# A new order table and named rooms for two kinds of turning tiles in an attention and gated feed-forward kernel

## The chip, the cores and the metric

The kernel runs on one core of a Trainium2 chip. The metric is the device time of one launch in microseconds, as the median of several executions. In the rows, PE is the matrix engine, PEld its weight loads, DVE the vector engine, ACT the scalar engine, POOL the GpSimd engine, and SP the engine that only issues transfers here (its transfers stand as SPq).

## The reference

Attention over keys and values that are averaged in groups of eight, and then a gated feed-forward layer on its output:

```
k_p = k.reshape(B, H, Sp, 8, D).mean(axis=3)      # B = H = 8, S = 576, D = 64, Sp = 72
v_p = v.reshape(B, H, Sp, 8, D).mean(axis=3)
attn = softmax(q @ k_p^T / sqrt(D))
x = (attn @ v_p) as 4608 tokens x 512
out = (sigmoid(x @ w_gate) * (x @ w_val)) @ w_out  # 512 x 1536, 512 x 1536, 1536 x 512, all float32
```

## The kernel before

The 4608 tokens are nine blocks of 512. Every float32 product is made of three products of a high and a low half (fp32r), so each operand is split: ACT copies the high half, DVE subtracts it from the original for the low one. The weights come from memory as 64-bit numbers, 1 MB for each of twelve pieces, and are converted on the chip by ACT and DVE (`to_f32`: two ACT steps w<-raw and raw<-raw, then DVE steps on w, then the split into `parts`).

The first pass (block 0's whole path, and the attention of blocks 1 and 2) is written out by hand in the string `ORDER`; it fills the first 140 us or so and converts all the weights on the way. After it come four rounds of two blocks each. A round makes gate and value products by a scheme of seven block products instead of eight (`hidden`, tiles `chain`), multiplies them into `h`, and makes the output products in the same way (`second_sums`, tiles `acc`). The attention of later blocks (`attention`: scores `sc`, exponentials `e`, transposes `tp`, products with the values `av`) is slipped in between, as tasks.

What is written is not issued at once: a `Book` records each instruction, or each group that must stay together, as one of 3800 numbered units. At the end the loop over the string `LATER` issues the units in the order of the numbers in it, and each engine gets its own share of them in that order. An engine works through its share strictly in turn, so a unit that has to wait holds up all that stand behind it on that engine. Tiles carry the dependencies: an instruction waits for what it reads, and the first write to a room waits for the last reader of what was there.

Two kinds of tiles turn in rings. `raw` tiles (128 x 576 float32, the landing place of keys, queries and values) come from the pool `rawp` with three rooms, in `load` (L593) and at the start of `first_pass`. `y` tiles (128 x 512 float32; gates of the first blocks in `gate` and `gated`, sums in `product`, outputs `o` in `result`) come from `two`, with two rooms for the tag `y`. A ring hands its rooms out in rotation, in the order in which the tiles are recorded. All recorded instructions carry the line of the recording helper, L317 (L320 after the change), so the rows are told apart by their tiles.

Of the kernel before, what the change touches and what calls it, by code (L numbers as in the profile page):

```python
# [11 lines left out]
F32 = mybir.dt.float32  # L12
# [7 lines left out]
P = 128  # L20
# [90 lines left out]

LATER = """
# [217 lines left out]
def attention_then_ffn(ctx: ExitStack, tc: tile.TileContext, qT, kT, vm, vr, vn, sums8, wgv, wo, const, out, outT):  # L330
# [34 lines left out]
    def split(h, l, x):  # L365

        nc.scalar.copy(h, x)
        nc.vector.tensor_tensor(out=l, in0=x, in1=h.bitcast(F32), op=ALU.subtract)

    kept = {
        (kind, p, g): dram.tile([P, 2, 2 * HALF], F32R, name=f"kept{kind}{p}{g}")
# [1204 lines left out]
```

## Time and profile before

| what | before |
| --- | --- |
| median of three runs | 906.28 us (904.79 to 907.96) |
| profiled execution, its own time | 906.25 us |
| its span, first to last instruction | 904.5 us |
| PE busy | 893.6 us (99%), 4162 matmuls |
| PEld, DVE, ACT, POOL busy | 81%, 73%, 55%, 22% |
| granted clock of PE | 1.000 in all slices |
| bytes moved | 237.56 MB, 263 GB/s over the span |

The time of the run is 1.75 us more than the span: this lies ahead of the first instruction and behind the last. A row of the profile gives the start, the length, the engine, the tile written and the tiles read, and in brackets the idle time of that engine just before it and what ended it. The ends of matmuls are modelled, and matmuls overlap, so a short stall of PE shows less idle time than it costs; the distance between the starts of two rows shows all of it.

### The profile page before, as it was taken

The numbers are of one execution on the slowest core, as the hardware profiler recorded it, in microseconds if no ns is written. First come the engines' busy times: TensorE is split into PE (matmuls) and PEld (weight loads), VectorE is DVE, ScalarE is ACT, GpSimd is POOL, SyncE is SP. The second block draws the span as 40 slices with busy tenths as digits, with TensorE's granted clock in tenths as the row PEclk, the third lists the DMA queues.
The fourth block names the chain that finished last, engine by engine and source line by source line (L and its number), as shares of the span: only waits on it lengthen the run. The fifth ranks groups of instructions, "written<-read, shape, count | busy, mean of one in ns | idle before, by whom it ended". The sixth has DMA issues, their size and how long they took to land.

```text
span 904.5 us, 12612 instructions
## 1 busy us (share of the span) xinstructions
PE 893.6 (99%) x4162; PEld 735.1 (81%) x4162; DVE 657.4 (73%) x1039; ACT 497.1 (55%) x1071; POOL 199.4 (22%) x369
## 2 busy tenths in 40 slices
PE   7999999999999999999999999999999999999998
PEld 6788778888888888888888888888888888888886
DVE  7989788889899998757678796356589552224863
ACT  5888887587856475445365554334355542224352
POOL 2412101011164235443343104132213000000000
PEclk9999999999999999999999999999999999999999
DMA  9899888889999888787987787686747775746644
GB/s 342 302 332 349 289 331 303 299 280 330 329 328 313 278 288 287 234 304 260 302 273 245 243 279 260 225 269 198 256 127 249 247 251 201 227 169 205 195 167 141
DMA packets 100289, 237.56 MB, mean 263 GB/s; under 512 B 13856, under 2 KB 34720, under 8 KB 98688
## 3 DMA queue, kind: packets, MB, share of 16 engines
q1 hardware_dynamic: 85040, 203.84, 66.7%
q0 software_dynamic: 15040, 32.79, 10.6%
q8 instruction: 33, 0.54, 0.2%
q14 instruction: 32, 0.26, 0.1%
q10 hardware_dynamic: 144, 0.13, 0.0%
HBM read 176.02 MB, written 60.69 MB: 262 GB/s over the span
## 4 chain that ended last, share of the span: by engine, by line
PE 90%; DVE 4%; DMA 3%; ACT 2%; issue 1%; SPq 0%; DVEq 0%; ACTq 0%
PE chain L317 55%; PE acc L317 27%; PE av L317 4%; PE sc L317 3%; DVE early L317 1%; DMA raw<-in_wgv 1%; DMA raw_o<-in_wo 1%; PE tp L317 1%; DMA raw<-in_vr 1%; DMA h<-in_kT 0%; ACT e L317 0%; DVE s L317 0%; DVE hs L317 0%; DVE h L317 0%; ACT hs L317 0%
## 5 line engine op out<-in xcount | busy, mean ns | idle before, releaser
L317 PE MATMUL chain<-xo,parts 128*128 128x512 f32 x2316 | 543.7, 392 | 0.0
L317 PEld LDWEIGHTS chain<-xo,parts 128*128 128x128 f32 x2316 | 430.7, 188 | 92.5 <-issue 1.0
L317 PE MATMUL acc<-hs,oparts 128*128 128x512 f32 x1008 | 237.3, 391 | 0.3 <-issue 0.2
L317 PEld LDWEIGHTS acc<-hs,oparts 128*128 128x128 f32 x1008 | 188.0, 188 | 40.9 <-issue 1.2
L317 POOL DMA_DIRECT2D turned<-turn x240 | 131.7, 551 | 214.8 <-DVE turn L317 185.2
L317 DVE TENSOR_TENSOR y<-chain,sV 128x512 f32<-128x512 f32 x46 | 31.1, 686 | 69.3 <-PE chain L317 59.0
L317 DVE TENSOR_TENSOR hs<-h,hs 128x1024 fp32r<-128x1024 f32 x52 | 63.0, 1217 | 11.6 <-ACT hs L317 11.4
L317 ACT CAST hs<-h 128x1024 fp32r<-128x1024 f32 x52 | 54.4, 1050 | 30.0 <-PE acc L317 23.1
L317 ACT COPY chain<-chain 128x512 f32<-128x512 f32 x46 | 26.4, 576 | 57.0 <-PE chain L317 47.3
L317 DVE TENSOR_TENSOR y<-chain,sG 128x512 f32<-128x512 f32 x46 | 31.2, 682 | 34.0 <-PE chain L317 23.4
L317 ACT CAST hs<-s 128x1024 fp32r<-128x1024 f32 x36 | 37.5, 1051 | 28.4 <-PE acc L317 13.0
L317 ACT COPY sG<-chain 128x512 f32<-128x512 f32 x46 | 26.7, 586 | 46.5 <-PE chain L317 44.8
L317 DVE TENSOR_TENSOR hs<-s,hs 128x1024 fp32r<-128x1024 f32 x36 | 43.8, 1219 | 11.2 <-ACT hs L317 10.9
L317 ACT COPY sV<-chain 128x512 f32<-128x512 f32 x46 | 26.7, 585 | 38.8 <-PE chain L317 36.1
L317 DVE SCALAR_TENSOR_TENSOR h<-gate,chain 128x512 f32<-128x512 f32 x46 | 30.6, 677 | 21.8 <-PE chain L317 21.7
L317 ACT ACTIVATE gate<-chain 128x512 f32<-128x512 f32 x46 | 26.9, 594 | 34.2 <-PE chain L317 31.7
L317 PE MATMUL sc<-kbd,raw 128*128 128x144 f32 (+1 forms) x262 | 41.2, 296 | 0.1
L317 PEld LDWEIGHTS sc<-kbd,raw 128*128 128x128 f32 (+1 forms) x262 | 33.6, 176 | 7.9 <-issue 2.8
L317 ACT ACTIVATE gate<-y 128x512 f32<-128x512 f32 x46 | 28.9, 633 | 19.1 <-DVE y L317 19.0
L317 PE MATMUL acc<-oparts,hs 128*128 128x512 f32 x144 | 38.7, 402 | 0.2 <-ACT oparts L317 0.2
L317 DVE TENSOR_REDUCE m<-sc 128x4 f32<-128x288 f32 x48 | 21.7, 452 | 18.2 <-PE sc L317 17.7
L317 DVE SCALAR_TENSOR_TENSOR h<-gate,y 128x512 f32<-128x512 f32 x46 | 31.0, 683 | 0.3
(211 smaller groups left out, 1073.8 us busy)
## 6 DMA issues: line engine op xcount, KB each, us to landing
oparts<-keptS SPq DMA_DIRECT2D x48, 512.0 KB, 4.4
oparts<-keptO SPq DMA_DIRECT2D x72, 256.0 KB, 4.2
raw<-in_wgv SPq DMA_DIRECT2D x12, 1024.0 KB, 8.5
out<-o SPq DMA_DIRECT2D x35, 256.0 KB, 3.6
raw<-in_kT SPq DMA_DIRECT2D x28, 288.0 KB, 5.0
raw<-in_qT SPq DMA_DIRECT2D x29, 256.0 KB, 4.7
raw<-in_vm SPq DMA_DIRECT2D x24, 256.0 KB, 5.6
raw_o<-in_wo SPq DMA_DIRECT2D x12, 512.0 KB, 8.1
```

Source lines behind the costliest of these rows:

```text
L317: return self._book.take(lambda: f(*args, **named))
```

## The change

The table `LATER` is replaced by another order of the same 3800 units. 707 of PE's 916 units stand at another place of PE's sequence, 922 of 1039 on DVE, 828 of 942 on ACT, 300 of 348 on POOL and 483 of 555 on SP; the mean move is 2.7, 4.7, 4.3, 2.7 and 3.6 places, the largest 43. No instruction is added, removed or resized.

Two strings now say which room a turning tile gets. `RAWS` has 77 digits for three rooms, and names the same room twice in a row 24 times; `YS` has 132 digits for two rooms, and does so 46 times. The rooms are as many and as large as before.

```
+RAWS = (
+    "12001221110021020122201202110021110020221001211220110020012211020100211102"
+)
+YS = (
+    "0101011001011001010101011100011000101010101000100110101110100111010110101100011110111010011001011011"
+    "10110010000110101001101001011101"
+)
 LATER = """
-6 5 4 7 0 11 3 2 21 8 25 27 19 28 14 18 23 31 22 20 9 26 13 35 17 36 33 1 10 40 45 76 39 37 12 48 47 52 16 55 32 66 38
...
+6 2 21 27 4 28 35 5 19 7 26 11 0 3 18 8 9 13 14 31 39 25 20 23 17 22 36 66 10 40 45 52 1 33 32 67 48 53 12 62 58 76 38
...
-    cpool, work, two = sb("cpool"), sb("work"), sb("two", 2)
-    rawp, wpool, opool = sb("rawp", 3), sb("wpool"), sb("opool")
+    cpool, work, two, ypool = sb("cpool"), sb("work"), sb("two", 2), sb("ypool")
+    rawp, wpool, opool = sb("rawp"), sb("wpool"), sb("opool")
...
+    raws, ys = iter(RAWS), iter(YS)
+
+    def raw_tile():
+        return rawp.tile([P, S], F32, name="raw", tag=f"raw{next(raws)}")
+
+    def y_tile(name):
+        return ypool.tile([P, BT], F32, name=name, tag=f"y{next(ys)}")
...
-        return fill(rawp.tile([P, S], F32, name="raw"), *what)
+        return fill(raw_tile(), *what)
...
-            y = two.tile([P, BT], F32, name="y", tag="y")
+            y = y_tile("y")
...
-        gate = two.tile([P, BT], F32, name="y", tag="y")
+        gate = y_tile("y")
...
-                t = two.tile([P, BT], F32, name="o", tag="y")
+                t = y_tile("o")
...
-        rooms += [rawp.tile([P, S], F32, name="raw") for _ in range(3)]
+        rooms += [raw_tile() for _ in range(3)]
...
-            ygate[f] = two.tile([P, BT], F32, name="y", tag="y")
+            ygate[f] = y_tile("y")
```

Three places of the new order matter below. The numbers behind tile names count buffers and are higher by three after the change.

The first is ACT's sequence in the first pass, around the conversion of an output weight (w_o and raw_o, then its high half oparts). The rows `e` are the exponentials of block 2, `hs` is the high half of block 0's h. Before:

```order
L317 ACTIVATE y<-chain 128x512
L317 ACTIVATE e,early<-sc,early 128x72
L317 ACTIVATE w_o<-raw_o 128x1024
L317 ACTIVATE e,early<-sc,early 128x72
L317 ACTIVATE raw_o<-raw_o,cst 128x1024
L317 ACTIVATE e,early<-sc,early 128x72 x5
L317 CAST hs<-h 128x1024
L317 ACTIVATE e,early<-sc,early 128x72 x4
L317 CAST oparts<-w_o 128x2x512
```

After:

```order
L320 ACTIVATE e,early<-sc,early 128x72 x4
L320 ACTIVATE y<-chain 128x512
L320 CAST vh_100<-early 64x64
L320 ACTIVATE w_o<-raw_o 128x1024
L320 ACTIVATE e,early<-sc,early 128x72 x2
L320 ACTIVATE raw_o<-raw_o,cst 128x1024
L320 CAST hs<-h 128x1024
L320 ACTIVATE e,early<-sc,early 128x72 x2
L320 CAST oparts<-w_o 128x2x512
```

The tanh of a gate (y<-chain), one copy of values (vh) and four exponentials now stand ahead of the conversion's first step, and between hs and oparts two exponentials are left of four.

The second is ACT's sequence some 40 rows later, where the last gate and value weights are converted (w_394 and raw_382 before are w_397 and raw_385 after; w_396 and raw_384 are the value weight's). Before:

```order
L317 CAST parts<-w_379 128x2x256
L317 ACTIVATE w_394<-raw_382 128x1024
L317 ACTIVATE raw_382<-raw_382,cst 128x1024
L317 ACTIVATE y<-chain 128x512
L317 CAST parts<-w_394 128x2x256 x2
L317 ACTIVATE y<-chain 128x512
L317 ACTIVATE kbd_91<-ks 64x72
L317 ACTIVATE w_396<-raw_384 128x1024
```

After:

```order
L320 ACTIVATE y<-chain 128x512 x2
L320 ACTIVATE w_397<-raw_385 128x1024
L320 ACTIVATE raw_385<-raw_385,cst 128x1024
L320 ACTIVATE kbd_94<-ks 64x72
L320 ACTIVATE w_399<-raw_387 128x1024
L320 CAST parts<-w_397 128x2x256
L320 ACTIVATE raw_387<-raw_387,cst 128x1024
L320 CAST other<-early 96x64
```

Both gates now stand ahead of the conversion of the gate weight, and the second step of its split (parts<-w_397) is moved behind the first two steps of the value weight and more.

The third is PE's sequence in the first round, where the products av of block 3's second pair follow the transposes tp of their probabilities pm. Before:

```order
L317 MATMUL tp<-cst,pm 128x128 x4
L317 MATMUL chain<-xo_459,parts 128x512 x6
L317 MATMUL chain<-xo_453,parts 128x512 x6
L317 MATMUL chain<-xo_467,parts 128x512 x6
L317 MATMUL chain<-xo_424,parts 128x512 x6
L317 MATMUL chain<-xo_416,parts 128x512 x6
L317 MATMUL av<-ph,vh_98 128x192
L317 MATMUL av<-pl,vh_98 128x192
L317 MATMUL av<-ph,vl_103 128x192
L317 MATMUL av<-pr,vres_108 128x192
L317 MATMUL av<-ph,vh_97 128x320
```

After:

```order
L320 MATMUL tp<-cst,pm 128x128 x4
L320 MATMUL chain<-xo_419,parts 128x512 x6
L320 MATMUL chain<-xo_420,parts 128x512 x6
L320 MATMUL chain<-xo_427,parts 128x512 x6
L320 MATMUL sc<-kbd_94,raw 128x144 x2
L320 MATMUL av<-ph,vh_101 128x192
L320 MATMUL av<-pl,vh_101 128x192
L320 MATMUL av<-ph,vl_106 128x192
L320 MATMUL av<-pr,vres_111 128x192
L320 MATMUL chain<-xo_419,parts 128x512 x6
L320 MATMUL av<-ph,vh_100 128x320
```

One more group of six chain matmuls and two score groups stand ahead of the first of the av rows, fewer of the others between the transposes and it.

## Rows read from the trace of the kernel before

**Rows 1.** The page, busy time, share of the span and count of each engine

```profile
PE 893.6 (99%) x4162; PEld 735.1 (81%) x4162; DVE 657.4 (73%) x1039; ACT 497.1 (55%) x1071; POOL 199.4 (22%) x369
```

**Rows 2.** Busy time by stretches: stretch, its length, each engine, clock, DMA share, GB/s

```profile
0.00:20.00 20.00, 15.75 (x82) 13.39 (x82) 14.93 (x37) 10.77 (x25) 3.67 (x22) 1.00 0.94 332
20.00:100.00 80.00, 79.40 (x390) 64.17 (x390) 72.01 (x121) 67.47 (x174) 21.08 (x29) 1.00 0.91 323
...
320.00:880.00 560.00, 559.98 (x2552) 462.38 (x2552) 364.37 (x522) 254.16 (x442) 123.45 (x225) 1.00 0.72 238
```

**Rows 3.** PE's timeline, the start-up

```profile
9.74 1.25 PE L317 MATMUL sc<-kbd,h 128*128 128x144 f32 x8 [1.16 <-ACT kbd L317]
...
14.72 0.55 PE L317 MATMUL tp<-cst,early 128*128 128x128 f32 x3 [0.92 <-DVE early L317]
...
20.42 0.63 PE L317 MATMUL tp<-cst,early 128*128 128x128 f32 x4 [0.57 <-DVE r L317]
```

**Rows 4.** PE's timeline, 98 to 101 us

```profile
98.44 0.65 PE L317 MATMUL sc<-kbd,raw 128*128 128x144 f32 x4
99.03 0.76 PE L317 MATMUL sc<-kbd,raws 128*128 128x144 f32 x4
99.97 1.19 PE L317 MATMUL acc<-oparts,hs 128*128 128x512 f32 x4 [0.18 <-ACT oparts L317]
```

**Rows 5.** ACT's timeline, 92 to 96 us

```profile
92.78 1.13 ACT L317 ACTIVATE w_o<-raw_o 128x1024 f32<-128x1024 f32 x1 [1.94 <-DMA raw_o<-in_wo]
...
95.24 0.30 ACT L317 ACTIVATE e<-sc,early 128x72 f32<-128x72 f32 x1
```

**Rows 6.** Timelines of PE and ACT, 105 to 110 us

```profile
105.50 0.59 ACT L317 COPY xs<-av 128x512 f32<-128x512 f32 x1
...
105.62 0.26 PE L317 MATMUL tr<-identr,r 128*96 128x128 f32 x1 [0.16 <-ACT early L317]
...
109.08 0.69 PE L317 MATMUL acc<-oparts,hs 128*128 128x512 f32 x2
109.91 0.76 PE L317 MATMUL sc<-kbd,raw 128*128 128x144 f32 x4
```

**Rows 7.** PE's timeline, 110 to 124 us

```profile
110.85 11.14 PE L317 MATMUL chain<-xo,parts 128*128 128x512 f32 x48
121.83 0.51 PE L317 MATMUL av<-early,vh 128*128 128x384 f32 x2
122.18 0.34 PE L317 MATMUL av<-early,vl 128*128 128x384 f32 x1
122.36 0.34 PE L317 MATMUL av<-pr,vres 96*128 96x384 f32 x1
123.41 0.66 PE L317 MATMUL tp<-cst,early 128*128 128x128 f32 x4 [0.72 <-ACT y L317]
```

**Rows 8.** ACT's timeline, 118 to 123 us

```profile
118.17 1.12 ACT L317 ACTIVATE w<-raw 128x1024 f32<-128x1024 f32 x1 [1.48 <-DMA raw<-in_wgv]
...
121.72 1.14 ACT L317 CAST parts<-w 128x512 fp32r<-128x512 f32 x2 [0.81 <-DVE w L317]
122.77 0.59 ACT L317 ACTIVATE y<-chain 128x512 f32<-128x512 f32 x1
```

**Rows 9.** Timelines of PE and DVE, 205 to 212 us

```profile
205.71 5.15 PE L317 MATMUL chain<-xo,parts 128*128 128x512 f32 x22
211.39 0.33 PE L317 MATMUL av<-ph,vh 128*128 128x192 f32 x1 [0.54 <-DVE pl L317]
...
210.56 0.68 DVE L317 TENSOR_TENSOR pl<-tp,ph 128x512 fp32r<-128x512 f32 x1
```

**Rows 10.** DVE's timeline, 18 to 19 us

```profile
18.78 0.29 DVE L317 TENSOR_TENSOR vres<-vr,vres 32x128 fp32r<-32x128 f32 x1
```

**Rows 11.** The chain of waits around 110 us: start, length, what

```profile
109.54 8.61 DMA raw<-in_wgv
```

**Rows 12.** The tile raw, its transfers' time from issue to landing

```profile
DMA to landing us min/median/max: 2.0/5.4/11.9
```

More of the change, by code (lines that the diff above doesn't have):

```diff
@@ L109 @@
 """
-LATER = """
[155 rows of a table removed]
+RAWS = (
+    "12001221110021020122201202110021110021020221001211220110020012211020100211102"
+)
[3 more added lines that the diff above has]
+)
+LATER = """
[150 rows of a table added]
 """
```

303 rows, old and new, of the table LATER are left out of this document.

## The prediction, made before the changed kernel ran

> **What bounds the kernel now.** I read the busy times first: PE is busy 893.6 of 904.5 us, so all other engines have room on the mean and only 10.9 us of PE's time are idle [rows 1]. The table by stretches says where: 4.25 us in the first 20 us, 0.60 in the next 80, and 0.02 in the 560 us from 320 to 880 [rows 2]. From 320 us on there is nothing for another order to take. What can be won lies in the first 300 us. There PE is not alone: from 20 to 100 us DVE is busy 72.01 of 80 us and the transfer engines 0.91 of the time [rows 2].
>
> Then I read PE's timeline in those 300 us, for rows that begin late. Two measures are needed, since a short stall hides behind the modelled ends. In dense work 48 matmuls of 512 columns start within 121.83 - 110.85 = 10.98 us, so one takes 0.229 us [rows 7]. A row that starts later than its predecessor's matmuls need at this pace has lost the difference, whatever idle time is printed.
>
> **What is lost there now.**
> - Start-up: the score matmuls wait 1.16 us for ACT's keys, and transposes wait 0.92 and 0.57 us for DVE's products [rows 3].
> - At 99.97 the output products of block 0 start 0.94 us after four score matmuls, where four alike took 0.59: 0.35 lost, for ACT's high half of the output weight [rows 4].
> - At 109.91 two matmuls of 512 columns have taken 0.83 us instead of 0.46: 0.37 lost [rows 6].
> - At 123.41 the transposes start 1.05 us after the last av matmul, where the same form before took 0.18: 0.87 lost, for a tanh on ACT (y) that frees their bank [rows 7].
> - At 211.39 the av product starts 5.68 us after 22 chain matmuls that need 22 x 0.229 = 5.04: 0.64 lost, for DVE's pl [rows 9].
>
> **The change, step by step.** No operation, byte or matmul is added or removed, so the cost is only in waits. I followed each stall into the new order.
>
> *At 122 us, -0.87.* The tanh that frees the bank runs at 122.77. Ahead of it on ACT stand the first two conversion steps of the last gate weight, which begin only at 118.17 after a wait of 1.48 us for the weight, and its split, which waits 0.81 more for DVE [rows 8]. In the new order both gates stand ahead of all that. Their chain products end well before 121.83, so the bank is free when the transposes come. The whole 0.87 goes if nothing else comes late. What may: the next chain product reads one of the two parts of that weight's split, and the ACT half of this part now stands behind the value weight's first step, which I take at the gate weight's 1.12. Of these, 0.81 fill the wait for DVE that was there anyway, so 0.31 is added; in return only one part, half of the 1.14, is needed first, so it is ready 0.57 - 0.31 = 0.26 us earlier than both were [rows 8]. PE comes 0.87 earlier. Bounds: 0, if the chain had been ready for it only just, and -0.87. The profile prints no wait of the chain for that split, so I take -0.87.
>
> *At 99 us, -0.35.* ACT sits 1.94 us idle at 92.78 for the weight, with exponentials queued behind [rows 5]. The new order runs four of them, a gate and a copy of values in that idle time, and leaves two instead of four between hs and oparts. Each is 0.30 us [rows 5], so oparts comes some 0.6 us earlier, more than the 0.35. Bounds: 0 and -0.35; I take -0.35, as 0.6 covers it.
>
> *At 105 and 109 us, +0.30 and -0.37.* On ACT the copy of the rest's probabilities (r from rest) moves from four exponentials ahead of the copy xs to behind it and one more exponential; its transposes now wait for up to one such copy, 0.59 us [rows 6]. PE stands at that place with 0.16 of wait already. Bounds 0 and +0.59; I take half, +0.30. The remaining transposes of the same tile and the copy after them then stand earlier than before, and the scores at 109.91 no longer wait: -0.37, bounds 0 and -0.37.
>
> *At 211 us, -0.64.* PE now does one more group of six chain matmuls (1.37 us) and two score groups ahead of the av rows, which is more than the 0.64 that it waited for pl. DVE's pl starts at 210.56 [rows 9], and stands two units earlier in DVE's sequence, so I let it run at the same time. Bounds 0 and -0.64; I take all.
>
> *Start-up, -0.30.* The product whose transposes PE waits for at 20.42 now stands ahead of a correction of 0.29 us [rows 10] and of another short product, which would save most of the 0.57 of [rows 3]. ACT's order around it also changed, and its copies feed the same rows, so I take half of the two, 0.30; bounds 0 and -0.57. The two earlier waits of 1.16 and 0.92 I leave: the keys and the products that they wait for stand no earlier by more than a place.
>
> *The tail, 0.* The last output piece is finished in the other order of its two halves; one half is evacuated in two parts by two engines, the other whole. Which one is last changes little: I take nothing, with 0.3 either way.
>
> *The rooms, 0.* A room named by hand lets a transfer start when that room's last reader is done, where the ring made it wait for the oldest of three. Where the new order reads the tiles out of turn this frees transfers earlier, and where the same room is named twice in a row it delays them. A landing in raw takes 5.4 us in the median [rows 12], and these loads are issued some units ahead of their readers. I take 0 as cover: PE and ACT work of at least this length lies between issue and reader at the places that I followed. If the cover is gone, the cost is the third rival below. The Trainium skill (Trainium Kernel Development and Optimization, Best Practices) says to double-buffer for performance, so that transfers overlap with compute; a room named twice in a row gives that up for these tiles. By that rule each of 24 such loads would show part of its landing, and the kernel would be slower; no row of before shows this case.
>
> *The sum:* -0.87 - 0.35 + 0.30 - 0.37 - 0.64 - 0.30 = -2.23 us on the 906.25 of the profiled execution, 904.0. Its own time is 0.03 below the median of the three runs, which makes no difference.
>
> **The rivals.**
>
> *More goes than I followed.* If the new start-up also removes the first two waits, 1.16 + 0.92 = 2.08 us [rows 3], the time is 906.25 - 2.23 - 2.08 = 901.9. For it: nearly every unit of the first 300 us was moved, and I followed only the stalls that I could name; losses of 0.1 to 0.3 us that print no idle time are many there. Against it: the first keys and queries come from memory and cannot come earlier.
>
> *The order does nothing that lasts.* The first 300 us are bound not by PE alone but by DVE (72.01 of 80 us) and the transfers (0.91) [rows 2]. A stall of PE that is removed then comes back some us later, when PE waits for the same DVE queue or the same weight. The time stays at about 906.2. For it: the stalls at 99, 122 and 211 all wait for ACT or DVE. Against it: from 140 us on PE's lead over DVE is several us.
>
> *A weight comes late: slower.* SP issues its transfers in turn. In the new order two small landings in raw rooms (keys and values) and a store stand ahead of the two 1 MB weight fetches that they stood behind. If the room named for one of these is still being read, SP waits, and the fetches behind it too. The last fetch has no slack: it is issued at 109.54, ACT starts on it 8.61 us later [rows 11] and had waited 1.48 us for it [rows 8], and PE's chain after 124 us reads what comes out. If SP's wait is as long as one landing, 5.4 us [rows 12], the time is 906.25 - 2.23 + 5.4 = 909.4. It decides from about 2.2 us of lateness on, where the gains are used up. Against it: ACT idles at this place, so the stores ahead are done early.
>
> **How the numbers follow.** My forecast, 904.0, has a chance of 0.42; its own range is 902.7 to 905.3, by the sum of the halves taken (0.30 at 105 us, 0.30 at start-up, 0.3 at the tail, and one of the smaller terms). The first rival has 0.27, the second 0.19, the third 0.12. A measurement of this kernel tells some 0.3% from no change, that is 2.7 us, so faster means below 903.5. All of the first rival and 0.17 of the forecast's 0.42 lie there: 0.44. The other 0.25 and the second rival are within 0.3%: 0.44. The third rival gives slower, 0.12. The range reaches from 900.8, some 1.1 below the first rival's time, to 907.5, above the second rival's with the runs' own scatter; it leaves out the third rival and the low end of the first, under 0.2.
>
> **What would show it.** In the changed kernel's timeline the transposes after the av rows near 122 us start without a wait for y; PE's idle time between 100 and 140 us falls by about 1; oparts near 98 us is done before PE's scores end; the av product near 211 us starts with no wait for pl; the transposes near 20 us start about 0.3 earlier; a new wait of 0.3 for ACT's r near 105 us. From 320 us on all distances stay as they are. I am wrong if PE's chain near 124 us starts later than before against the block before it (the weight is late), if new waits for DMA of raw appear on DVE or ACT, or if the whole gain shows in the first 20 us.

## The result, and the profile after

The changed kernel takes 913.09 us (912.28 to 913.72, 4 runs), before takes 906.79 beside it (904.79 to 907.96, 4 runs): the ratio is 1.0071, 95% interval 1.0051 to 1.0092. It is 6.3 us slower, where 904.0 was predicted and the range ended at 907.5. The profiled execution took 913.72, with a span of 911.9.

The page's busy times of the changed kernel, the line that answers to [rows 1]:

```profile
PE 894.8 (98%) x4162; PEld 735.1 (81%) x4162; DVE 660.6 (72%) x1039; ACT 497.2 (55%) x1071; POOL 209.9 (23%) x369
```

PE does the same work, 894.8 against 893.6 us, and the span is 7.4 longer: PE waits more. The table by stretches of the changed kernel, with the columns of [rows 2], tells where:

```profile
0.00:20.00 20.00, 14.37 (x80) 12.39 (x81) 13.89 (x34) 9.44 (x22) 3.67 (x22) 1.00 0.92 328
20.00:100.00 80.00, 78.21 (x380) 62.33 (x379) 72.10 (x122) 67.17 (x170) 25.59 (x26) 1.00 0.93 322
100.00:140.00 40.00, 40.00 (x205) 33.23 (x204) 36.05 (x61) 37.74 (x95) 5.21 (x9) 1.00 0.90 331
140.00:220.00 80.00, 78.69 (x388) 64.97 (x387) 68.23 (x128) 53.68 (x156) 14.21 (x20) 1.00 0.84 288
220.00:320.00 100.00, 99.15 (x464) 80.84 (x464) 93.69 (x165) 69.06 (x185) 38.66 (x70) 1.00 0.91 312
320.00:880.00 560.00, 556.35 (x2533) 458.81 (x2532) 360.53 (x518) 248.81 (x436) 122.57 (x224) 1.00 0.72 238
```

And the three stretches of before that stood in no rows yet:

```profile
100.00:140.00 40.00, 38.98 (x188) 31.43 (x189) 32.58 (x54) 35.58 (x87) 2.15 (x4) 1.00 0.88 331
140.00:220.00 80.00, 79.44 (x394) 64.88 (x393) 71.70 (x140) 55.38 (x161) 10.87 (x20) 1.00 0.85 296
220.00:320.00 100.00, 99.92 (x476) 82.88 (x476) 92.47 (x161) 66.89 (x179) 38.16 (x70) 1.00 0.92 311
```

PE's idle time is the length less the first number. It changes by +1.38, +1.19, -1.02, +0.75, +0.77 and +3.63 us. Only 100 to 140 us won, where three of the followed stalls lie; more than half of the added idle time is behind 320 us, where the prediction had expected nothing at all.

PE's timeline of the changed kernel shows the gains and the new stalls. The numbers in brackets are idle time and what ended it. The first chain row, at 28.93, stands for the start-up; in before it is

```profile
27.29 2.99 PE L317 MATMUL chain<-xo,parts 128*128 128x512 f32 x12
```

The changed kernel:

```profile
8.66 1.22 PE L320 MATMUL sc<-kbd,h 128*128 128x144 f32 x8 [1.65 <-DMA h<-in_qT]
10.94 1.22 PE L320 MATMUL sc<-kbd,h 128*128 128x144 f32 x8 [1.06 <-DMA h<-in_qT]
...
28.93 2.32 PE L320 MATMUL chain<-xo,parts 128*128 128x512 f32 x9
...
53.76 0.47 PE L320 MATMUL acc<-oparts,hs 128*128 128x512 f32 x1 [0.88 <-DVE r L320]
...
98.78 0.65 PE L320 MATMUL sc<-kbd,raws 128*128 128x144 f32 x4
99.17 2.11 PE L320 MATMUL acc<-oparts,hs 128*128 128x512 f32 x8
...
124.22 0.34 PE L320 MATMUL av<-pr,vres 96*128 96x384 f32 x1
124.40 0.38 PE L320 MATMUL tp<-cst,early 128*128 128x128 f32 x2
...
208.65 0.76 PE L320 MATMUL sc<-kbd,raw 128*128 128x144 f32 x4 [1.31 <-ACT e L320]
...
213.81 0.65 PE L320 MATMUL sc<-kbd,raw 128*128 128x144 f32 x4
214.21 0.35 PE L320 MATMUL av<-ph,vh 128*128 128x192 f32 x1
...
334.87 1.43 PE L320 MATMUL acc<-hs,oparts 128*128 128x512 f32 x5 [0.89 <-DMA oparts<-keptO]
...
368.14 4.18 PE L320 MATMUL chain<-xo,parts 128*128 128x512 f32 x16 [1.29 <-DVE xo L320]
...
402.28 1.89 PE L320 MATMUL chain<-xo,parts 128*128 128x512 f32 x7 [0.85 <-DVE y L320]
```

The transposes behind the av rows start 0.18 us after them, not 1.05 [rows 7]; the output products start 0.39 after four score matmuls, not 0.94 [rows 4]; the av rows near 214 us follow without a wait [rows 9]. Against that stand stalls at 208, 334, 368 and 402 us that before has nowhere. What stands ahead of them is on other engines. DVE's timeline of the changed kernel:

```profile
207.28 0.68 DVE L320 TENSOR_REDUCE vs<-raw 96x64 f32<-96x512 f32 x1 [2.76 <-DMA raw<-in_vr]
...
366.27 0.71 DVE L320 STREAM_TRANSPOSE turn<-pm 128x512 f32<-128x512 f32 x1 [2.73 <-DMA turned<-turn]
366.90 1.18 DVE L320 TENSOR_TENSOR xo<-s,xo 128x1024 fp32r<-128x1024 f32 x1
...
397.18 0.71 DVE L320 STREAM_TRANSPOSE turn<-pm 128x512 f32<-128x512 f32 x1 [4.39 <-DMA turned<-turn]
...
401.54 0.69 DVE L320 TENSOR_TENSOR y<-chain,sV 128x512 f32<-128x512 f32 x1
```

A transpose writes the tile `turn`, whose room POOL's transfers are still reading, and DVE stands still for 2.73 and 4.39 us. Behind the transpose are queued the low half of xo and the y on which PE waits: xo ends at 368.08 and PE starts at 368.14. SP's queue of the changed kernel has the same pattern at the two other stalls:

```profile
198.18 0.59 SPq L320 DMA_DIRECT2D raw<-in_vr  x1
198.81 0.61 SPq L320 DMA_DIRECT2D w<-keptWO  x1
199.47 0.46 SPq L320 DMA_DIRECT2D raw<-in_vr  x1
...
326.90 0.56 SPq L320 DMA_DIRECT2D raw<-in_kT  x1
327.51 0.53 SPq L320 DMA_DIRECT2D oparts<-keptO  x1
```

A 512 KB weight stands ahead of the last piece of the values that DVE needs at 207 us (it waits 2.76 for them), and a load of keys ahead of the weight that PE needs at 334.

DVE's waits, grouped (us in total, times, longest), are the shortest sign of the change, though not its price: the longest of them, 4.7 us, has no wait of PE behind it. Changed kernel:

```profile
DVE turn L320 <- DMA turned<-turn: 18.7, 6, 4.7
```

Before:

```profile
DVE turn L317 <- DMA turned<-turn: 2.5, 2, 1.8
```

The tile raw, its landings in the changed kernel, against [rows 12]:

```profile
DMA to landing us min/median/max: 1.8/4.7/10.7
```

### The profile page after: what moved, and what is told of

The parts are those of the page before. It is cut to its first block, busy times and chain, and to the rows that moved or that the text cites. A ratio compares the mean times of both kernels' runs of the same rounds, so it can differ in the third digit from the quotient of the medians.

```text
span 911.9 us, 12630 instructions
## 1 busy us (share of the span) xinstructions
PE 894.8 (98%) x4162; PEld 735.1 (81%) x4162; DVE 660.6 (72%) x1039; ACT 497.2 (55%) x1071; POOL 209.9 (23%) x369
## 4 chain that ended last, share of the span: by engine, by line
PE 73%; DMA 6%; issue 5%; POOL 4%; DVE 4%; ACT 2%; SPq 0%; DVEq 0%; POOLq 0%; ACTq 0%
PE chain L320 41%; PE acc L320 26%; POOL turned L320 3%; DMA turned<-turn 3%; PE av L320 3%; PE sc L320 3%; DMA raw<-in_vr 1%; DMA oparts<-keptO 1%; DMA w<-keptWO 1%; ACT e L320 1%; DVE turn L320 1%; PE tp L320 1%; DMA w<-keptwV 0%; SPq L320 0%; DVE h L320 0%
```

## The experiments

Theory A: the new order alone costs the time, by local stalls that add up. Theory B: the named rooms hold transfers back. Theory C: nothing new is lost, the gains are given back later. In the mixtures, a unit's place in time is that of its row in before, and rooms go to the first one free. Each ratio is to the executions of before that ran beside that kernel, whose medians were 906.21 to 906.63 for the kernels below "changed". "Idle" is PE's idle time from 320 to 880 us in the one profiled execution, "turn" DVE's wait for the room of turn in it. The profiled executions of r_lru (908.40) and late (909.26) were the fastest of their six, 3.9 and 2.8 below the medians, so these two columns do not stand for the median there.

| kernel | median us (runs) | ratio to before, 95% | idle | turn |
| --- | --- | --- | --- | --- |
| before | 906.79 (4) | | 0.02 | 2.5 |
| changed | 913.09 (4) | 1.0071 (1.0051 to 1.0092) | 3.65 | 18.7 |
| r_lru | 912.32 (6) | 1.0058 (1.0039 to 1.0077) | 0.93 | 12.2 |
| h_start | 912.15 (6) | 1.0056 (1.0042 to 1.0070) | 1.67 | 14.8 |
| h_mid | 906.30 (12) | 1.0003 (0.9993 to 1.0014) | 0.00 | 2.5 |
| moves | 909.12 (8) | 1.0028 (1.0014 to 1.0042) | 0.73 | 6.8 |
| late | 912.06 (6) | 1.0073 (1.0060 to 1.0086) | 2.35 | 15.1 |
| h_end | 906.85 (12) | 1.0009 (0.9999 to 1.0018) | 0.37 | 6.1 |
| gates | 911.20 (5) | 1.0055 (1.0043 to 1.0067) | 0.00 | 3.0 |
| gates2 | 905.59 (12) | 0.9990 (0.9981 to 1.0000) | 0.30 | 2.2 |
| mid_90_150 | 904.88 (11) | 0.9986 (0.9977 to 0.9994) | 0.00 | 2.6 |
| mid_211 | 904.90 (12) | 0.9987 (0.9977 to 0.9997) | 0.00 | 4.6 |
| plant | 914.03 (6) | 1.0074 (1.0050 to 1.0097) | 5.32 | 12.7 |
| r_last | 931.72 (6) | 1.0278 (1.0240 to 1.0316) | 11.98 | 17.9 |

### The rooms: r_lru and r_last

```diff
 RAWS = (
-    "12001221110021020122201202110021110021020221001211220110020012211020100211102"
+    "12001221110021020122201202110021110021020221101210221001122101100212022100021"   # r_lru
+    "12022000112101110212101120002102222021020212002211002121002222010020102120001"   # r_last
```

(YS likewise.)

> The changed kernel with its order table untouched; only the two strings are replaced, so that each raw and y tile takes the room that came free first. Theory A, that the order alone makes the loss: 913 us, within 0.7 of the changed kernel, with the same waits near 208, 334, 366 and 401 us. Theory B, that named rooms hold transfers back: those waits shrink, and the time is 908 to 910 us.

912.32: the loss stays. Its profiled execution, at 908.40, has only two of the four waits that were expected: PE waits 1.54 us at 207.46 and 0.71 at 333.08, but not near 366 and 401. The first of the two transposes did not wait there:

```profile
361.68 0.69 DVE L320 STREAM_TRANSPOSE turn<-pm 128x512 f32<-128x512 f32 x1
```

The order is the same, so which of its places cost something differs with the naming or between executions; which of the two, one trace cannot tell. The room that is free longest is nearly the one that the change names (in the order of use, raw repeats 7 times against 8, y 27 against 26), so the median shows that the naming adds little, not that rooms are harmless. That was tried by the opposite.

> The changed order as it is, but each turning tile is given, of the rooms that are free at its place, the one that was given up last, so that in the order of use the same raw room comes twice in a row 15 times instead of 8, and the same y room 66 times instead of 26. Theory A (the order alone costs the time; the rooms leave slack): 912 to 914 us, and the waits for landings in raw stay near the 4.3 us of the changed kernel. Theory B (a room named again at once holds its transfer or its gate back, and that costs time): as the repeats double, the loss of 6 us grows by half or more, 916 us and above.

931.72: my expectation by theory A is wrong by 18 us. The rooms have no slack to speak of; DVE waits 4.6 us for keys and 4.6 for values in raw, PE 1.5 for queries in raw, and a y for ACT's gate 13.8 instead of 8.2. So theory B names a real cost, but not that of this change: with rooms given to the first free one, the new order still loses 6 us, and before's order is not slower (gates2, mid_90_150). In the changed kernel's trace, all waits for landings in raw come to 4.3 us (values 3.3, keys 0.8, weights 0.2), as many as before's 4.3 (2.0 for values, 2.3 for weights).

### Where the loss lies: h_start, h_mid, late, h_end

```diff
-LATER = order of the change
+LATER = order of before to 27 us, of the change behind                    # h_start
+LATER = order of before to 75 us, of the change to 200, of before behind  # h_mid
+LATER = order of before to 204 us, of the change behind                   # late
+LATER = order of the change to 200 us, of before behind                   # h_end
```

> The old order for all units that ran in the first 27 us of the kernel before, the new order for the rest, rooms by first free. Theory A, local losses that add up: the first chain matmul comes at 27.3 us instead of 28.9, and 1.6 us of the loss go: 911.5 us. Theory C, that what is won at one place comes back at the next because DVE and the transfers bound the first 300 us: the 1.6 us are gone by 130 us and the time stays at 913 us.

912.15, no better than r_lru. In its profile another wait for queries stands at the start (1.40 us at 6.73), and from 10 to 15 us the granted clock is 0.80, where before's is 1.00. What the new start-up costs stays open.

> The old order for units that ran before 75 us and after 200 us in the kernel before, the new order only for those between, rooms by first free. Theory A: the gains at 99, 105 to 109 and 122 us (2.3 us between 75 and 125 us in the changed kernel, some 0.9 more up to 200 us) stay, the losses ahead and behind are gone: 903.5 to 904.5 us, about 2.5 below the kernel before. Theory C: the gains come back as waits behind 200 us: 906 to 907 us.

906.30, as theory C had it, but not for its reason. 100 to 140 us keep their gain, and 320 to 880 have no idle time; PE's timeline of h_mid shows new waits at the seam, where the two orders meet:

```profile
74.83 1.65 PE L320 MATMUL chain<-xo,parts 128*128 128x512 f32 x6 [0.88 <-ACT xs L320]
...
77.51 0.70 PE L320 MATMUL chain<-xo,parts 128*128 128x512 f32 x2 [0.54 <-DVE h L320]
79.55 0.74 PE L320 MATMUL chain<-xo,parts 128*128 128x512 f32 x2 [1.34 <-DVE parts L320]
```

The first of the three may not be the seam's: gates (below), which has none, waits 1.00 us for xs at 75.39. The other two come to 1.88 us.

> Before's order for all units that ran before 204 us in the kernel before, the changed order for all behind; rooms given to the first free one. The start-up, the gains at 99 to 122 us and the load that came late for the 208 us stall are all before's. Theory A (the new order brings stalls of its own, each local, and they add up): the stalls of the changed kernel behind 225 us stay, which are 1.7 us (225 to 275) and 5.3 us (325 to 425) more than before, so 911.5 to 914 us. Theory C (nothing is lost behind 200 us; what was gained at 99 to 122 us is given back there): nothing was gained, so nothing is given back, 906 to 907.5 us.

912.06: 5.8 us more than before, though nothing had been gained that could be given back. Theory C falls. A rival that the theories leave out, a lower clock, falls for this part of the loss: four of the six executions ran at a mean granted clock of 1.000 and took 909.26 to 912.58. In the profiled one the waits at 334 and 368 are missing, that at 402 is down to 0.42 (at 396.87), and the same pattern stands at a place where the changed kernel's profile has no wait of PE. DVE's timeline of late, and PE's:

```profile
443.86 0.71 DVE L320 STREAM_TRANSPOSE turn<-pm 128x512 f32<-128x512 f32 x1 [4.49 <-DMA turned<-turn]
...
445.94 0.73 PE L320 MATMUL sc<-kbd,raw 128*128 128x144 f32 x4 [1.93 <-DVE e L320]
```

The e that PE waits for is queued behind the transpose.

> The complement: the changed order for all units that ran before 200 us, before's order for all behind. Theory A: the changed kernel's gains (3.2 us between 75 and 200 us) and its losses in the first 75 us (2.8 us) stay and nearly cancel, the stalls behind 200 us go; with up to 1 us for the seam 905.5 to 907.5 us. Against it, a loss that comes from the first 200 us (the late start-up, weights that land late) and shows only later: 909 to 912 us, since the first 200 us are those of the changed kernel.

906.85: 0.6 more than before. The two halves add up, 5.8 + 0.6 = 6.4, to the 6.3 of the change, each known to about 1 us.

### Taking four waits out of the changed kernel: moves

On SP, two loads back behind those they had passed; on DVE, two transposes behind what PE needs. Two of the four:

```diff
 L320 DMA oparts<-keptO_194 128x2x256
-L320 DMA raw<-in_kT 128x576
 L320 DMA oparts<-keptO_196 128x2x256
+L320 DMA raw<-in_kT 128x576

 L320 TENSOR_REDUCE m<-sc 128x4
-L320 STREAM_TRANSPOSE turn<-pm 128x512
 L320 TENSOR_TENSOR xo_831<-s,xo_831 128x1024
 L320 TENSOR_REDUCE ks<-raw 128x72
 L320 TENSOR_TENSOR xo_827<-xs_661,xo_827 128x1024
+L320 STREAM_TRANSPOSE turn<-pm 128x512
```

> The changed kernel with four single moves, rooms by first free: on SP the 512 KB load of w4 behind the last piece of the value remainder (wait at 208 us, 1.48 us), on SP a 288 KB load of keys behind the load of oparts (wait at 334 us, 1.06), and on DVE two transposes into the tile turn behind the work that PE waits for (waits at 366 us, 1.45, and at 401 us, 1.02). Theory A: each of the four waits goes or nearly goes: 908 to 909.5 us. Theory B or C: the waits stay or turn up elsewhere: 911 to 913 us.

909.12. The kernel that differs by the four moves alone is r_lru, with the same way of giving rooms, and it took 912.32: 3.2 us come back, though the two intervals just overlap (1.0014 to 1.0042 and 1.0039 to 1.0077), and 2.9 us of loss to before are left. The stalls at 208, 334, 368 and 402 us are gone from the profile, but those at 368 and 402 were missing in r_lru's as well, so what each move is worth is not shown. A new wait stands at 289.86, 1.04 us for an output weight.

### Putting two waits into the kernel before: plant

```diff
 TENSOR_TENSOR e<-sc,m 128x288
+STREAM_TRANSPOSE turn<-pm 128x512
 TENSOR_TENSOR xo<-s,xo 128x1024
 TENSOR_TENSOR xo<-xs,xo 128x1024
...
-STREAM_TRANSPOSE turn<-pm 128x512
```

(and the other such transpose ahead of a y)

> Before's order with two single moves on DVE, those that the changed order makes near 366 and 397 us: the transpose of pm into turn stands ahead of the low half of xo, and the other such transpose ahead of a y. Nothing else differs. Theory A (a transpose placed ahead holds DVE until POOL's transfers have read turn out, and PE waits for what is queued behind it): in the kernel before the last of those transfers is issued at 358.20, and in the changed kernel such a transfer frees the room 4.6 us after its issue, so the transpose waits until 362.3 to 362.9 and the low half of xo is done at 364.2 to 364.8 instead of 360.77, with PE ready for it at 360.76: 3.4 to 4.0 us lost; the second pair costs 0.4 to 0.8. So 909.5 to 911 us. If PE's own lead and DVE's slack absorb the wait (the changed kernel's loss has another cause): 906 to 907 us.

914.03, 7.6 us lost: theory A's mechanism, and about twice its size. DVE's timeline of plant:

```profile
364.68 0.71 DVE L320 STREAM_TRANSPOSE turn<-pm 128x512 f32<-128x512 f32 x1 [4.88 <-DMA turned<-turn]
```

And PE's:

```profile
361.24 0.48 PE L320 MATMUL chain<-xo,parts 128*128 128x512 f32 x1
366.55 7.93 PE L320 MATMUL chain<-xo,parts 128*128 128x512 f32 x23 [4.83 <-DVE xo L320]
374.32 0.65 PE L320 MATMUL sc<-kbd,raw 128*128 128x144 f32 x4
```

One matmul takes 0.229 of the 5.31 us up to 366.55, so 5.08 are lost in the wait; then 23 matmuls take 7.77 instead of 23 x 0.229 = 5.27, and 2.50 more are lost. Plant by stretches (the number ahead of the DMA share is the granted clock):

```profile
368.00:370.00 2.00, 2.00 (x6) 1.61 (x5) 0.91 (x2) 0.00 (x0) 1.98 (x5) 0.50 0.61 154
374.00:380.00 6.00, 6.00 (x32) 4.66 (x31) 3.69 (x7) 2.83 (x6) 1.10 (x2) 1.00 0.69 222
```

After the long wait PE runs at a granted clock of 0.50, 1.2 GHz, and is back at 1.00 by 374. The Trainium skill (TensorE: Matmul & The Clock Gate, What's actually happening) says that an array that has been idle is passed every second pulse until activity releases it; the trace agrees, with 0.50. Two of the six executions took 909.5, at a mean clock of 0.998; the other four took 914.0 to 915.6 at 0.994 to 0.995. The two lie at the lower end of what was expected, so what was missing in the expectation is probably the clock's share; neither was traced. The second transpose waited 4.92 us, at 402.07, and cost PE 0.49, as expected.

### The prediction's own terms: gates, gates2, mid_90_150, mid_211

```diff
 ACT, 118 us: +y<-chain x2 ahead of w<-raw of the last gate weight
 ACT, 93 us:  +e<-sc,early x3 ahead of w_o<-raw_o
 PE, 211 us:  +chain<-xo,parts x6 ahead of av<-ph,vh
 PE, 211 us:  +sc<-kbd,raw x2 ahead of av<-ph,vh         # gates alone
```

> Before's order with only seven single moves, those on which three terms of the prediction rest: on ACT both gates ahead of the last gate weight's first step (the stall at 123 us, 0.87), three exponentials into the idle time ahead of the output weight's first step (99 us, 0.35), on PE six chain matmuls and a score group ahead of the av rows at 211 us (0.64). If the terms hold and last: 906.25 - 1.86, so 904.0 to 904.9 us. If stalls that are taken away come back at the next wait for ACT, DVE or a weight (theory C): 905.8 to 907 us.

911.20, 5 us slower. The seventh move did it, as gates2 shows. SP's queue of gates:

```profile
211.04 0.33 SPq L320 DMA_DIRECT2D raw<-in_qT  x1
```

And PE's timeline:

```profile
215.90 0.77 PE L320 MATMUL sc<-kbd,raw 128*128 128x144 f32 x4 [2.90 <-DMA raw<-in_qT]
```

The score group was put ahead of the landing of its own queries; behind it, from 218 to 219 us, the granted clock is 0.50 here too.

> The seven single moves without the seventh, the score group that was put ahead of the av rows at 211 us and there waited 2.90 us for its queries (loaded at 210.67 in the order before, at 197.79 in the changed one). Six chain matmuls remain ahead of the av rows. If the prediction's terms for 99, 123 and 211 us hold and last: 904.0 to 904.9 us. If they come back: 905.8 to 907 us. If the 5 us that the seven moves lost did not come from that one wait: 908 to 911 us.

905.59: without that move the 5 us are gone, and the six others win 0.8 us, the interval reaching from nothing to 1.7, of the 1.86 forecast. PE's timeline of gates2 has neither the stall at 123 nor the one at 211:

```profile
122.72 0.34 PE L320 MATMUL av<-pr,vres 96*128 96x384 f32 x1
122.90 0.60 PE L320 MATMUL tp<-cst,early 128*128 128x128 f32 x4
...
203.29 8.44 PE L320 MATMUL chain<-xo,parts 128*128 128x512 f32 x36
211.56 0.25 PE L320 MATMUL av<-ph,vh 128*128 128x192 f32 x1
```

For the two mixtures:

```diff
+LATER = order of before to 90 us, of the change to 150, of before behind   # mid_90_150
+  and PE's six chain matmuls ahead of av<-ph,vh at 211 us                  # mid_211
```

> Before's order, with the changed order only for the units that ran between 90 and 150 us in the kernel before. Theory A: the gains at 99 to 123 us (2.3 us) stay, start-up and the part behind 150 us are before's, and the seam stalls of the earlier mixture at 73 to 78 us (3.3 us) are not there: 903.5 to 905 us. Theory C: 906 to 907 us.

904.88, faster than both kernels: 1.3 us less than the 906.22 of before beside it. The part of the new order that the prediction had read best is worth having, alone.

> The mixture with the changed order between 90 and 150 us, and on PE the six chain matmuls ahead of the av rows at 211 us. Theory A: 904.9 less the 0.64 that PE waits there, 904.0 to 904.6 us; if that wait is given back, 904.7 to 905.2 us.

904.90, the second outcome. The term brings nothing on top: in the profile of mid_90_150 the av rows there start without a wait already.

## Why the prediction was wrong

**The step that failed** is "I followed each stall into the new order", with its premise "From 320 us on there is nothing for another order to take": the cost of the new order at places without a stall was put at nothing. That nothing can be won in a stretch with 0.02 us of idle time is true; the prediction drew from it that "all distances stay as they are". An order that moves most of the units can lose there, and it did: 3.63 us of idle time between 320 and 880, and 5.8 us behind 204 (late). I followed the stalls that existed and no place that had none. One of the prediction's own signs of being wrong came: a new wait of DVE for a landing in raw, 2.76 us at 207.28.

**What stands in its place.** On an engine or queue that works strictly in turn, the order put a unit that waits for a transfer (a landing, or the read-out of its room) ahead of one that PE needs next. Taking four such units back won 3.2 us (moves against r_lru); putting two of them into before cost 7.6 (plant), where the wait was longer and the clock fell. The Trainium skill (PSUM — Partial Sum Buffer, Engine vs sequencer instructions) calls the queues of ScalarE, VectorE and GpSimdE strict FIFO; the trace agrees for VectorE, with 4.39 us in which DVE stands still ahead of one transpose. Nearly half of the loss, 2.9 us, is left in moves. The stalls at 53 us and from 265 to 272 and the start-up were read in the trace, not tried one by one, and the places that cost something differ between the traces of changed, r_lru and late, so the loss is not shown place by place.

**The terms.** -0.87, -0.35 and -0.37 came: 100 to 140 us lost its 1.02 of idle time, and the +0.30 for r did not show there. Their mixture won 1.3 us (0.5 to 2.1) of these 1.59; gates2 won 0.8 (nothing to 1.7) of 1.86. Whether the terms were oversized or partly given back is not shown. -0.64 at 211 came too, but the same stretch of the new order put 1.31 of wait at 208.65, for values that land late. The start-up term has the wrong sign: the first chain starts at 28.93 against 27.29, 1.64 later. I had read DVE's sequence near 19 us and not SP's, where the keys, queries and constants stand in another order; PE's first two waits there are for queries. As h_start won nothing, what it is worth in the median is open.

**The rooms, 0,** was right for this naming and wrong in its reason. The cover of "at least this length" does not hold in general: with the rooms of r_last the same order takes 18.6 us more than the changed kernel. The names in the change are close to the first free room, and with that naming itself (r_lru) the time is the same within the scatter. The 24 repeats that the prediction counted are in the order of recording; in the order of use the change takes a raw room twice in a row only 8 times. The Trainium skill's rule on double-buffering (Trainium Kernel Development and Optimization, Best Practices), which the prediction set beside this term, agrees in direction with r_last, where raw rooms repeat 15 times and y rooms 66 times in the order of use; for the change it would have misled. The sentence ahead of the prediction that a ring hands its rooms out in rotation is also too simple: in the program built from before, too, raw tiles take the same room twice in a row.

**The rivals.** "A weight comes late" had the right family, a queue held by a transfer, with 909.4 and a chance of 0.12, and was tied to one place, 109 us, where nothing happened. "Nothing lasts" fell with late as a cause of the loss. "More goes than I followed" failed in the start-up, where PE's first two waits are 1.65 and 1.06 us instead of shorter ones.

## What to carry to other kernels

Before a reordering is priced, list in the new order, for each engine and queue, the units that wait for a transfer or for a room that a transfer still reads, and what PE needs from behind them; the places without a stall today are where the loss can be. One profiled execution does not show all of them: the same order had its waits at other places in other traces. In a kernel that is 99% dense a new order has much to lose and little to win: keep the stretch where it helps, and before's order elsewhere. A load and its reader must move together: a reader moved ahead alone cost 5 us here.

## What was not expected of the hardware

A wait of PE can cost more than its length: 2.50 us at a granted clock of 0.50 followed a wait of 4.83, and the same clock followed one of 2.90. The length of a wait alone does not tell: those up to 1.65 in the profile of the changed kernel were followed by 1.00, but in that of moves, which has the same order in its start-up, PE waited 1.56 us at 8.27 and then ran at half clock though it was busy 4.36 of 5 us (moves by stretches):

```profile
10.00:15.00 5.00, 4.36 (x18) 3.67 (x17) 4.80 (x13) 1.30 (x4) 0.00 (x0) 0.50 1.03 405
```

The mean clock of the changed kernel's four executions was 0.995 to 0.999, and only the one at 0.999 was traced, so what its start-up cost in the others is open. The time from issue to landing of POOL's transfers out of turn (median 4.5 us in before, near this place) is nearly what most of the transposes shown wait, 4.39 to 4.88; one waits 2.73. And executions of one kernel differ by more than the terms argued over: before took 904.18 to 909.12 in 23 runs.
